# The first layer of a softplus feed-forward network by Strassen's scheme over pairs of weight tiles

## The chip, the cores and the metric

The kernel runs on one core of a Trainium2 chip. Its engines are named as the profile names them: PE is TensorE's matmul stream and PEld its weight loads, DVE is VectorE, ACT is ScalarE, POOL is GpSimd, and SP is the engine whose queue issues the transfers. Each engine works its own instructions off in the order in which they were written, and waits on semaphores for the others. The metric is the time of one execution on the device in microseconds (us).

## What is computed

Eight batches of 576 tokens go through a decaying causal attention without softmax (8 heads of 64), and the result through a feed-forward network with softplus between its layers:

```
scores = q @ k.T / sqrt(64);  ret = scores * gamma[h] ** (i - j) for i >= j, else 0
x = (ret @ v) as 4608 tokens x 512
h = x @ w_in            # 512 -> 2048, the first layer
g = max(h, 0) + log1p(exp(-abs(h)))
out = g @ w_out         # 2048 -> 512, the second layer
```

The weights arrive as 64-bit floats, two 32-bit words each.

## The kernel before

**Numbers in two parts.** Every operand of the two layers is held as a high part (the value as float32r) and a low part (what that leaves), and each product is the sum of three: low by high, high by low, high by high (`TERMS`).

**Units and slots.** The tokens form 9 units of 512 (`T`). A unit has 16 slots, one for each tile of 128 of the 2048 hidden values. In slot i, `hidden_mm` (L367) multiplies 12 times 512 columns: four pieces of the 512 inputs, three terms. ACT then takes Abs, Exp and Ln (L375 to L377), DVE adds the positive part (L383, L387), ACT writes the high part of g (L391) and DVE its low part (L395). `output_mm` (L407) of the slot before multiplies 12 times 512 columns, three for each of the four groups of 128 tokens (banks y0 to y3). So PE has 24 products of 512 columns in a slot, and each slot's elementwise work has the time of the slot after it.

**Attention.** A step m is half the heads of a chunk of 128 tokens. The first nine steps run in an opening of some 23 us. The others lie between the slots: up to slot 18 one step in every odd slot, then one chunk (two steps, `chunk_products`) ahead of every fourth slot. DVE scales what comes out (`values_out`, L346), ACT writes its high part and POOL its low part into the unit's input tile (L351, L352). POOL also scales the next step's v (`scale_values`, L151) once its transfer (`load_step`, tiles keys and qv) has landed.

**Weights.** In the 16 slots of unit 0 the two halves of each tile's weights are loaded, joined to float32 (L440, L447, L453) and split into high and low (L461, L466). They then stay in the core's memory, so that from unit 1 on nothing is loaded but attention's inputs.

**Order.** The order of the instructions is written out by hand, and each engine follows it. Tiles come from pools with a fixed number of buffers; a new tile waits until the last reader of its buffer's former tile is done.

## Time and profile before

| what | value |
|---|---|
| median of 3 timed runs | 892.06 us (892.0 to 892.66) |
| span of the profiled execution | 890.1 us |
| PE busy | 879.6 us (99%), 7634 matmuls |
| DVE, ACT, POOL busy | 460.1 (52%), 440.6 (49%), 144.1 us (16%) |
| products of the first layer (L367) | 1740, of 12 a slot |
| products of the second layer (L407) | 1728 |
| read and written in the chip's main memory (HBM) | 59.26 MB and 9.44 MB |

The profiled execution has no time of its own beside its span, which lacks 1.96 us to the median. Matmuls overlap, so the mean duration of one (391 ns) is longer than the distance between two; distances are read from rows of the timeline.

### The profile page before, as it was taken

To read this page: it belongs to the slowest core of one execution; us is meant where nothing else is said; L and a number is where in the kernel's file an instruction comes from. 1 tells how busy PE (TensorE), PEld (TensorE's weight loads), DVE (VectorE), ACT (ScalarE), POOL (GpSimd) and SP (SyncE) were. 2 spreads that over 40 slices of the span, in tenths; PEclk is the share of its full clock that TensorE was granted. 3 is DMA by queue.
4 is the path that set the end of the run, shared out by engine and by line. 5 is a ranking of instruction groups with operands and counts; after the bars stand their busy time and mean duration, and the time that the engine had idled before them with its cause. 6 is when DMAs were issued, how large, how long until landed. Compare 5 with 4: busy or idle time off the path is not lost.

```text
span 890.1 us, 18133 instructions
## 1 busy us (share of the span) xinstructions
PE 879.6 (99%) x7634; PEld 723.8 (81%) x7634; DVE 460.1 (52%) x875; ACT 440.6 (49%) x771; POOL 144.1 (16%) x265
## 2 busy tenths in 40 slices
PE   8999999999999999999999999999999999999998
PEld 6777778888888888888888888888888888888886
DVE  5898864445444454455444454444444544434333
ACT  6777854444544454444444454444444544444444
POOL 4221222111111111111111111111111111000000
PEclk9999999999999999999999999999999999999999
DMA  9666623111310121112111131012111211001001
GB/s 364 193 216 221 218 69 113 54 55 54 102 47 23 41 101 54 55 55 101 55 54 54 55 102 54 26 41 90 54 54 54 101 55 54 2 1 48 0 1 48
DMA packets 29313, 69.86 MB, mean 78 GB/s; under 512 B 3248, under 2 KB 3248, under 8 KB 29232
## 3 DMA queue, kind: packets, MB, share of 16 engines
q1 hardware_dynamic: 29232, 68.71, 22.9%
q8 instruction: 60, 0.98, 0.5%
q14 instruction: 21, 0.17, 0.1%
HBM read 59.26 MB, written 9.44 MB: 77 GB/s over the span
## 4 chain that ended last, share of the span: by engine, by line
PE 93%; DVE 3%; ACT 1%; DMA 1%; issue 0%; SPq 0%; DVEq 0%
PE h L367 43%; PE y L407 42%; PE sums L174 2%; PE bank L158 2%; PE bank L230 2%; PE bank L242 1%; DVE w L466 1%; DMA raw<-whole 1%; DVE g L395 1%; PE pair L290 1%; DMA wst<-w 1%; PE bank L327 0%; PE bank L305 0%; ACT ab L377 0%; ACT ab L376 0%
## 5 line engine op out<-in xcount | busy, mean ns | idle before, releaser
L367 PE MATMUL h<-xt,w 128*128 128x512 f32 (+1 forms) x1740 | 420.5, 391 | 1.9 <-DVE w L466 1.3
L407 PE MATMUL y<-w,g 128*128 128x512 f32 x1728 | 415.9, 390 | 1.2 <-DVE g L395 1.2
L407 PEld LDWEIGHTS y<-w,g 128*128 128x128 f32 x1728 | 323.7, 188 | 71.0 <-DVE g L395 4.0
L367 PEld LDWEIGHTS h<-xt,w 128*128 128x128 f32 x1740 | 322.1, 188 | 70.0 <-DVE w L466 1.7
L375 ACT ACTIVATE ab<-h 128x512 f32<-128x512 f32 (+1 forms) x145 | 86.3, 595 | 252.0 <-PE h L367 252.0
L383 DVE TENSOR_SCALAR r<-h 128x512 f32<-128x512 f32 x125 | 86.4, 692 | 211.1 <-ACT ab L375 211.1
L391 ACT CAST g<-ab 128x512 fp32r<-128x512 f32 (+1 forms) x145 | 89.5, 617 | 106.1 <-DVE ab L387 104.9
L395 DVE TENSOR_TENSOR g<-ab,g 128x512 fp32r<-128x512 f32 (+1 forms) x145 | 103.1, 711 | 69.4 <-ACT g L391 68.0
L352 POOL TENSOR_TENSOR xt<-x,xt 128x256 fp32r<-128x256 f32 x71 | 54.2, 780 | 519.7 <-ACT xt L351 519.7
L387 DVE SCALAR_TENSOR_TENSOR ab<-r,ab 128x512 f32<-128x512 f32 x125 | 89.4, 715 | 79.6 <-ACT ab L377 79.6
L376 ACT ACTIVATE ab<-ab 128x512 f32<-128x512 f32 (+1 forms) x145 | 91.2, 629 | 4.6
L377 ACT ACTIVATE ab<-ab 128x512 f32<-128x512 f32 (+1 forms) x145 | 91.2, 629 | 4.7
L351 ACT CAST xt<-x 128x256 fp32r<-128x256 f32 x72 | 27.1, 405 | 56.8 <-DVE x L346 55.4
L151 POOL TENSOR_TENSOR qv<-qv,consts_sb 128x256 f32<-128x256 f32 x61 | 41.3, 676 | 52.0 <-DMA qv<-others 51.6
L225 POOL TENSOR_TENSOR s<-s,consts_sb 128x128 f32<-128x128 f32 x55 | 24.2, 440 | 62.3 <-DVE s L223 50.1
L158 PE MATMUL bank<-qv,keys 64*64 64x64 f32 x976 | 34.0, 222 | 0.0
L346 DVE TENSOR_TENSOR x<-bank,consts_sb 128x256 f32<-128x256 f32 x64 | 24.6, 419 | 17.8 <-PE sums L174 12.3
L174 PEld LDWEIGHTS sums<-qv,keys 64*64 64x64 f32 x768 | 26.5, 134 | 8.5 <-issue 8.5
L230 PE MATMUL bank<-a,qv 64*64 64x64 f32 x976 | 32.9, 218 | 0.0
L158 PEld LDWEIGHTS bank<-qv,keys 64*64 64x64 f32 x976 | 29.4, 134 | 3.5 <-issue 3.5
L174 PE MATMUL sums<-qv,keys 64*64 64x64 f32 x768 | 32.0, 221 | 0.0
L230 PEld LDWEIGHTS bank<-a,qv 64*64 64x64 f32 x976 | 29.9, 135 | 0.4 <-issue 0.4
(84 smaller groups left out, 444.2 us busy)
## 6 DMA issues: line engine op xcount, KB each, us to landing
qv<-others SPq DMA_DIRECT2D x61, 320.0 KB, 4.1
wst<-w SPq DMA_DIRECT2D x32, 512.0 KB, 4.2
keys<-others SPq DMA_DIRECT2D x61, 256.0 KB, 3.5
out<-osb SPq DMA_DIRECT2D x36, 256.0 KB, 2.4
raw<-whole SPq DMA_DIRECT2D x7, 512.0 KB, 8.3
raw<-others SPq DMA_DIRECT2D x3, 576.0 KB, 10.7
part<-first SPq DMA_DIRECT2D x1, 512.0 KB, 3.7
part<-first SPq DMA_DIRECT2D x1, 262.0 KB, 2.7
```

What stands on the lines that cost most here:

```text
L158: nc.tensor.matmul(L["S"][rows[t], h, part[s]], L["k"][rows[h], s, part[t]], L["q"][rows[h], s, part[t]], start=True, stop=True, skip_grou ...
L174: nc.tensor.matmul(L["T"][rows[h], t, part[s]], L["kp"][rows[t], s, rows[h]], L["v"][rows[t], s, rows[h]], start=True, stop=True, skip_gro ...
L230: nc.tensor.matmul(L["O"][rows[h], t, part[s]], L["v"][rows[t], s, rows[h]], L["a"][rows[t], h, s], start=clear, stop=L["states"][t] is No ...
L367: nc.tensor.matmul(h, ws[p][:, a, kt * P:(kt + 1) * P], xt[:, b, kt, cols], start=(n == 0), stop=(n == 3 * NKT - 1))
L375: nc.scalar.activation(ab, h, AF.Abs)
L376: nc.scalar.activation(ab, ab, AF.Exp, scale=-1.0)
L377: nc.scalar.activation(ab, ab, AF.Ln, bias=1.0)
L383: nc.vector.tensor_scalar_max(r, h, 0.0)
L387: nc.vector.scalar_tensor_tensor(ab, h, 0.0, ab, op0=ALU.max, op1=ALU.add)
L391: nc.scalar.copy(g[:, HI], ab)
L395: nc.vector.tensor_sub(g[:, LO], ab, g[:, HI].bitcast(F32))
L407: nc.tensor.matmul(y, g[:, a, at:at + P], ws[p][:, b, PIECE:], start=(p == 0 and n == 0), stop=(p == NF - 1 and n == 2))
```

## The change

From unit 1 on, the first layer is no longer computed slot by slot, but for pairs of hidden tiles (64 pairs J, 8 for each unit) by Strassen's scheme in Winograd's form. The weights of a pair form 2 by 2 blocks (256 inputs by 128 hidden values), the unit's inputs 2 by 2 blocks (256 inputs by 256 tokens). Instead of 8 block products there are 7, each of 6 matmuls of 256 columns (two pieces of inputs, three terms): 42 matmuls of 256 columns where two slots had 24 of 512. Three of the sums are gathered by accumulating several products in one PSUM bank; between them ACT copies the partial sum out (`keep`) and DVE adds two of them into halves of two tiles hs, from which Abs, Exp and Ln now read. The output products of the former pair stand between the seven, in four portions (`fill_in`).

- **Inputs.** From unit 1 on, seven of the eight combinations of a chunk's halves are formed by POOL (`combined_out`), and ACT and POOL split all seven at once (`x_head`, `x_rest`).
- **Weights.** In unit 0 each joined first-layer tile is also written to a scratch in HBM (`plain`). In the last slot of unit 0 and during the first seven pairs of unit 1, two such tiles are read back into one buffer f (`combine_load`), combined by four POOL operations (`combine`), split by ACT and DVE in three groups ga, gb, gc (`combine_split`) and written to another scratch (`combined`). The pair that follows uses the blocks from where they were split. From unit 2 on, the blocks of a pair are read from the scratch two pairs ahead (`block_load`): 7 blocks of 256 KB, 1.8 MB a pair, into two buffers for each group.
- **The rest.** The separate positive part (L383) goes. The second layer's products, attention's products and their number stay as they were. The last slot is no longer cut in two.

What stands in the engines' queues, at three places. Rows name tiles without their numbers where they can be told without.

ACT in unit 1, before, two slots (ab and g are the elementwise tiles, h a PSUM bank):

```order
L375 ACTIVATE ab<-h 128x512 [waits PE_49]
L376 ACTIVATE ab<-ab 128x512 [waits Activation_49]
L377 ACTIVATE ab<-ab 128x512 [waits Activation_49]
L391 CAST g<-ab 128x512 [waits DVE_49]
L375 ACTIVATE ab<-h 128x512 [waits PE_49]
L376 ACTIVATE ab<-ab 128x512 [waits Activation_49]
L377 ACTIVATE ab<-ab 128x512 [waits Activation_49]
L391 CAST g<-ab 128x512 [waits DVE_49]
```

and with the change, one pair of unit 1 (kept are the copied sums, hx and hy the two PSUM banks, f the pair of weight tiles being combined, ga, gb, gc its groups):

```order
L717 COPY kept<-hx 128x256 [waits PE_49]
L717 COPY kept<-hy 128x256 [waits PE_49]
L546 CAST ga__1927<-f 128x768 [waits DMAHW6_49,DMAHW1_49,Pool_49]
L717 COPY kept<-hx 128x256 [waits DVE_49,PE_49]
L722 ACTIVATE ab<-hs 128x512 [waits DVE_49]
L723 ACTIVATE ab<-ab 128x512 [waits Activation_49]
L724 ACTIVATE ab<-ab 128x512 [waits Activation_49]
L546 CAST gb__1960<-f 128x512 [waits DMAHW7_49,Pool_49]
L431 CAST g<-ab 128x512 [waits DVE_49,PE_49]
L546 CAST gc__1980<-f 128x512 [waits DMAHW3_49,DMAHW0_49,Pool_49]
L787 COPY hs<-hx 128x4x64 [waits PE_49]
L722 ACTIVATE ab<-hs 128x512 [waits Activation_49]
```

The three casts from f stand between the copies and the logarithms of the pair, and behind POOL and the transfers.

DVE at the same place, before, two slots:

```order
L383 TENSOR_SCALAR r<-h 128x512 [waits Activation_49]
L387 SCALAR_TENSOR_TENSOR ab<-r,ab 128x512 [waits DVE_49,Activation_49]
L395 TENSOR_TENSOR g<-ab,g 128x512 [waits Activation_49]
L383 TENSOR_SCALAR r<-h 128x512 [waits Activation_49]
L387 SCALAR_TENSOR_TENSOR ab<-r,ab 128x512 [waits DVE_49,Activation_49]
L395 TENSOR_TENSOR g<-ab,g 128x512 [waits PE_49,Activation_49]
```

and with the change, the same pair:

```order
L752 TENSOR_TENSOR hs<-hy,kept 128x4x64 [waits Activation_49]
L435 TENSOR_TENSOR g<-ab,g 128x512 [waits DVE_49]
L376 TENSOR_TENSOR xb<-bank,consts_sb 128x256
L209 TENSOR_TENSOR a<-bank,mask 128x256
L547 TENSOR_TENSOR ga__1927<-f,ga__1927 128x768 [waits DMAHW6_49,DMAHW1_49,Activation_49]
L763 TENSOR_TENSOR hs<-hy,kept 128x4x64 [waits PE_49,Activation_49]
L547 TENSOR_TENSOR gb__1960<-f,gb__1960 128x512 [waits Activation_49]
L769 TENSOR_TENSOR hs<-hx,kept 128x4x64 [waits PE_49]
L427 SCALAR_TENSOR_TENSOR ab<-hs,ab 128x512 [waits DVE_49]
L547 TENSOR_TENSOR gc__1980<-f,gc__1980 128x512 [waits DMAHW3_49,DMAHW0_49,Activation_49]
L435 TENSOR_TENSOR g<-ab,g 128x512 [waits DVE_49]
```

The low parts of the three groups stand between the additions that empty the PSUM banks (the rows that write hs) and the softplus.

SP and POOL around the same pair; before, SP's loads of two steps and POOL's work for a chunk:

```order
L137 DMA keys<-others 128x512 [waits DMAHW5_49,DMAHW1_49,PE_49]
L140 DMA qv<-others 128x640 [waits DMAHW6_49,Pool_49]
L137 DMA keys<-others 128x512 [waits DMAHW3_49,PE_49]
L140 DMA qv<-others 128x640 [waits DMAHW0_49,Pool_49]
L137 DMA keys<-others 128x512 [waits DMAHW5_49,PE_49]
L140 DMA qv<-others 128x640 [waits DMAHW2_49,Pool_49]
```

```order
L352 TENSOR_TENSOR xt_1691<-x,xt_1691 128x2x128 [waits Activation_49] x2
L207 COPY sx<-s 64x128 [waits PE_49,Pool_49]
L225 TENSOR_TENSOR s<-s,consts_sb 128x128 [waits DVE_49,Pool_49]
L207 COPY sx<-s 64x128 [waits PE_49,Pool_49]
L225 TENSOR_TENSOR s<-s,consts_sb 128x128 [waits DVE_49,Pool_49]
L151 TENSOR_TENSOR qv<-qv,consts_sb 128x256 [waits DMAHW0_49]
L151 TENSOR_TENSOR qv<-qv,consts_sb 128x256 [waits DMAHW2_49,PE_49]
```

with the change, SP (wf is the scratch of plain tiles, the first three rows write the combined groups) and POOL:

```order
L548 DMA ga_125<-ga__1927 128x1536 [waits DMAHW2_49,DVE_49]
L548 DMA gb_126<-gb__1960 128x1024 [waits DMAHW3_49,DVE_49]
L548 DMA gc_127<-gc__1980 128x1024 [waits DMAHW4_49,DVE_49]
L529 DMA f<-wf_109 128x512 [waits DMAHW5_49,Pool_49]
L530 DMA f<-wf_110 128x256 [waits DMAHW6_49]
L531 DMA f<-wf_110 128x256 [waits DMAHW7_49]
L155 DMA keys<-others 128x512 [waits DMAHW0_49,PE_49]
L158 DMA qv<-others 128x640 [waits DMAHW1_49]
L155 DMA keys<-others 128x512 [waits DMAHW2_49,PE_49]
L158 DMA qv<-others 128x640 [waits DMAHW3_49]
```

```order
L243 TENSOR_TENSOR s<-s,consts_sb 128x128 [waits DVE_49] x2
L169 TENSOR_TENSOR qv<-qv,consts_sb 128x256 [waits DMAHW1_49,PE_49]
L169 TENSOR_TENSOR qv<-qv,consts_sb 128x256 [waits DMAHW3_49,PE_49]
L538 TENSOR_TENSOR f<-f 128x256 [waits DMAHW7_49,DMAHW6_49,Activation_49]
L538 TENSOR_TENSOR f<-f 128x256 [waits DMAHW5_49,Pool_49]
L538 TENSOR_TENSOR f<-f 128x256 [waits Pool_49]
L538 TENSOR_TENSOR f<-f 128x256
```

The reads into f now stand on SP behind the write of group gc and ahead of the loads of the next attention steps, and POOL's combining stands behind the scaling of v, which waits for those loads.

The diff, cut to its core:

```diff
+B11, B22, B21, T1, T3, T2, NT4 = range(7)
+GROUPS = {"ga": 3, "gb": 2, "gc": 2}
+A11, A12, S1 = (("ga", n) for n in range(3))
+S2, S4 = (("gb", n) for n in range(2))
+S3, A22 = (("gc", n) for n in range(2))
+FA21, FA11, FA12, FS1, FS2, FS4, FS3, FA22 = range(8)
+FGROUPS = {"ga": slice(1, 4), "gb": slice(4, 6), "gc": slice(6, 8)}
...
+    rawp, xpools, wpool, gpool = pool("rawp", 2), [pool("xeven", 1)], pool("wpool", 1), pool("gpool", 2)
...
+    plain = [dram.tile([P, PIECE], I32, name=f"wf{p}") for p in range(NF)]
+    combined = [{g: dram.tile([P, 2, n, 2 * P], F32R, name=f"{g}{j}") for g, n in GROUPS.items()} for j in range(NJ)]
...
+            shape = [P, 2, 7, 2, HT] if u else [P, 2, NKT, T]
+            xts[u] = xpools[u % 2].tile(shape, F32R, tag="xt", name=f"xt{u}")
...
+    def halves_out(m):
+        L = live.pop(m)
+        pr = 2 * (m % 2)
+        if m % 2 == 0:
+            xbs[0] = att.tile([P, 8, 2, HC], F32, tag="xb", name="xb", bufs=1)
+        nc.vector.tensor_mul(xbs[0][:, pr:pr + 2], L["O"].rearrange("p t (s c) -> p t s c", s=2),
+                             constant[0][2][:, pr:pr + 2].rearrange("p s (t c) -> p t s c", t=2))
+    def combined_out(m, engine):
+        xb = xbs[0]
+        if m % 2 == 0:
+            engine.tensor_sub(xb[:, 4], xb[:, 0], xb[:, 1])
+        else:
+            engine.tensor_sub(xb[:, 5:7], xb[:, 2].unsqueeze(1).broadcast_to([P, 2, 2, HC]), xb[:, 0:5:4])
+            engine.tensor_sub(xb[:, 7], xb[:, 3], xb[:, 6])
...
+    def x_head(ch):
+        nc.scalar.copy(x_parts(ch)[0], xbs[0][:, 1:8])
+    def x_rest(ch, engine):
+        hi, lo = x_parts(ch)
+        engine.tensor_sub(lo, xbs[0][:, 1:8], hi.bitcast(F32))
...
-        nc.vector.scalar_tensor_tensor(hi, hi, 3, lo, op0=ALU.logical_shift_left, op1=ALU.bitwise_or)
+        if n % 2 == 0:
+            full = wst.tile([P, PIECE], I32, tag="full", name="full", bufs=2)
+            nc.vector.scalar_tensor_tensor(full, hi, 3, lo, op0=ALU.logical_shift_left, op1=ALU.bitwise_or)
+            nc.sync.dma_start(plain[n // 2], full)
     def weight_dst(n):
-        cols = slice((n % 2) * PIECE, (n % 2 + 1) * PIECE)
-        return ws[n // 2][:, HI, cols], ws[n // 2][:, LO, cols]
+        p = n // 2
+        if n % 2:
+            return wouts[p][:, HI], wouts[p][:, LO]
+        if p not in wins:
+            wins[p] = gpool.tile([P, 2, PIECE], F32R, tag=("gb", "gc")[p % 2], name=f"win{p}")
+        return wins[p][:, HI], wins[p][:, LO]
+    def combine_load(j):
+        f = later["f"].tile([P, 8, 2 * P], I32, tag="f", name="f")
+        nc.sync.dma_start(f[:, FA11:FA12 + 1].rearrange("p b c -> p (b c)"), plain[2 * j])
+        nc.sync.dma_start(f[:, FA21], plain[2 * j + 1][:, 0:2 * P])
+        nc.sync.dma_start(f[:, FA22], plain[2 * j + 1][:, 2 * P:])
+        fulls["f", j] = f.bitcast(F32)
+    def combine(j):
+        f = fulls["f", j]
+        for out, a, op, b in ((FS1, FA21, nc.gpsimd.tensor_add, FA22), (FS2, FS1, nc.gpsimd.tensor_sub, FA11),
+                              (FS4, FA12, nc.gpsimd.tensor_sub, FS2), (FS3, FA11, nc.gpsimd.tensor_sub, FA21)):
+            op(f[:, out], f[:, a], f[:, b])
+    def place_block(j, g):
+        blocks[j, g] = gpool.tile([P, 2, GROUPS[g], 2 * P], F32R, tag=g, name=f"{g}_")
+        return blocks[j, g]
+    def combine_split(j, g):
+        f, t = fulls["f", j][:, FGROUPS[g]], place_block(NJ + j, g)
+        nc.scalar.copy(t[:, HI], f)
+        nc.vector.tensor_sub(t[:, LO], f, t[:, HI].bitcast(F32))
+        nc.sync.dma_start(combined[j][g].bitcast(F32), t.bitcast(F32))
+    def block_load(J, g):
+        if NJ * 2 <= J < NPAIRS:
+            nc.sync.dma_start(place_block(J, g).bitcast(F32), combined[J % NJ][g].bitcast(F32))
...
+    for i in range(NF):
...
+        if i == NF - 1:
+            combine(0)
...
+        def step_out():
+            halves_out(m - 1)
+            combined_out(m - 1, nc.vector if i == NF - 1 else nc.gpsimd)
             scores_out(m)
             states_out(m)
-            for k in (m + 1,) if i < by_chunks - 2 else (m + 1, m + 2):
-                load_step(k)
...
+            if m + 1 >= NOPEN:
+                load_step(m + 1)
+            scale_values(m + 1)
+        def parts_out():
+            if (m - 1) % 2:
+                x_head((m - 1) // 2)
+                x_rest((m - 1) // 2, nc.vector if i == NF - 1 else nc.gpsimd)
+        if i == NF - 1:
+            step_out()
+            parts_out()
...
-            for name, bufs in (("osb", 4), ("odd", 2), ("r", 1), ("mark", 2)):
+            for name, bufs in (("osb", 3), ("odd", 2), ("f", 1), ("mark", 2)):
                 later[name] = ctx.enter_context(tc.tile_pool(name=name + "2", bufs=bufs, side="right"))
+            combine_load(0)
+        if i == NF - 1:
+            for g in GROUPS:
+                combine_split(0, g)
+            combine_load(1)
...
+    groups = {NJ: ([m + 1], [m])}
+    m += 2
+    for J in (J for J in range(NJ + 1, NPAIRS) if J % NJ in ((1, 2, 4, 5) if J < 2 * NJ else (0, 2, 4, 5))):
+        groups[J] = [k for k in (m, m + 1) if k < NSTEP], [k for k in (m - 2, m - 1) if k >= groups[NJ][0][0]]
+        m += 2
...
+    def product(out, J, a, x, start):
+        g, n = a
+        w = blocks[J, g]
+        k = 0
+        for ta, tb in TERMS:
+            for kt in range(2):
+                nc.tensor.matmul(out, w[:, ta, n, kt * P:(kt + 1) * P], x_tile(J // NJ)[:, tb, x, kt],
+                                 start=start and k == 0, stop=k == 5, skip_group_check=True)
+                k += 1
...
+    def keep(part):
+        kept = moe.tile([P, HT], F32, tag="kept", name="kept")
+        nc.scalar.copy(kept, part)
+        return kept
...
+    late, last = [], None
+    for J in range(NJ, NPAIRS):
+        u, j = divmod(J, NJ)
+        if J == NJ:
+            fills = [[(NF - 1, (tt,))] for tt in range(CPU)]
+        else:
+            fills = [[(2 * J - 2, (0, 1))], [(2 * J - 2, (2, 3))], [(2 * J - 1, (0, 1))], [(2 * J - 1, (2, 3))]]
...
+        prep = u == 1 and j + 1 < NJ
+        tile_a, tile_b = (moe.tile([P, T], F32, tag="hs", name="hs") for _ in range(2))
+        if prep:
+            combine(j + 1)
+        X = ps_h.tile([P, T], F32, tag="h0", name="hx")
+        Y = ps_h.tile([P, T], F32, tag="h1", name="hy")
+        x0, y0, y1 = X[:, 0:HT], Y[:, 0:HT], Y[:, HT:]
+        product(x0, J, A11, B11, True)
+        p1 = keep(x0)
+        product(y1, J, A12, B21, True)
+        product(y0, J, S1, T1, False)
+        block_load(J + 2, "ga")
+        p5 = keep(y0)
+        nc.vector.tensor_add(half(tile_a, 1), by_chunk(y1), by_chunk(p1))
+        for f in late:
+            f()
+        late = []
+        if prep:
+            combine_split(j + 1, "ga")
+        fill_in(0)
+        product(x0, J, S2, T2, False)
+        u2 = keep(x0)
+        product(y0, J, S4, B22, False)
+        block_load(J + 2, "gb")
+        nc.vector.tensor_add(half(tile_a, 0), by_chunk(y0), by_chunk(u2))
+        ab = hidden_logs(tile_a)
+        if prep:
+            combine_split(j + 1, "gb")
+        fill_in(1)
+        product(x0, J, S3, T3, False)
+        nc.vector.tensor_add(half(tile_b, 0), by_chunk(x0), by_chunk(p5))
+        softplus(tile_a, ab)
+        if last is not None:
+            x_head(last)
+            x_rest(last, nc.gpsimd)
+            last = None
+        ga = softplus_split(ab)
+        gs[2 * J] = ga
+        if prep:
+            combine_split(j + 1, "gc")
+        fill_in(2)
...
+        product(x0, J, A22, NT4, False)
+        block_load(J + 2, "gc")
+        if u == 1 and j + 2 < NJ:
+            combine_load(j + 2)
+        nc.scalar.copy(half(tile_b, 1), by_chunk(x0))
+        softplus_rest(ga, ab)
+        if J in groups:
+            steps, done = groups[J]
+            chunk_products(steps, done)
+            for m in steps:
+                states_out(m)
+            def outs(steps=steps, done=done):
+                for m in done:
+                    halves_out(m)
+                    combined_out(m, nc.gpsimd)
+                for m in steps:
+                    scores_out(m)
+            late.append(outs)
+            if done and done[-1] % 2:
+                last = done[-1] // 2
+            for m in steps:
+                for k in (m + 1, m + 2) if J == NJ else (m + 2,):
+                    if k < NSTEP:
+                        load_step(k)
+                        scale_values(k)
+        fill_in(3)
...
+        ab = hidden_logs(tile_b)
+        softplus(tile_b, ab)
+        gb = softplus_split(ab)
+        gs[2 * J + 1] = gb
+        late.insert(0, lambda g=gb, ab=ab: softplus_rest(g, ab))
+    for f in late:
+        f()
+    output_mm(2 * J)
+    output_mm(2 * J + 1)
```

159 lines of the change are left out of this document (69 added, 90 removed).

## The prediction, made before the change was run

> **What bounds the kernel now.** I read the page's shares first, then the windows, which give the busy time of each engine in a stretch (the column behind the length is PE's), then the timeline for the distances.
>
> ```profile
> PE 879.6 (99%) x7634; PEld 723.8 (81%) x7634; DVE 460.1 (52%) x875; ACT 440.6 (49%) x771; POOL 144.1 (16%) x265
> ...
> 47.00:72.00 25.00, 24.59 (x224) 19.40 (x223) 22.74 (x43) 19.45 (x34) 6.43 (x8) 1.00 0.63 216
> 142.00:238.00 96.00, 96.00 (x869) 79.54 (x868) 47.07 (x93) 43.31 (x73) 16.16 (x29) 1.00 0.19 61
> ```
>
> From unit 1 on PE is busy in all of the 96 us; ACT and DVE have half of each stretch free. In unit 0 (47 to 72 us) DVE is at 91% and PE just short of full. So the time is PE's stream, and its unit is the distance between two products:
>
> ```profile
> 123.31 2.88 PE L367 MATMUL h<-xt,w 128*128 128x512 f32 x12
> ...
> 126.03 2.88 PE L407 MATMUL y<-w,g 128*128 128x512 f32 x12
> ...
> 877.44 3.05 PEld L367 LDWEIGHTS h<-xt,w 128*128 128x128 f32 x24
> 877.66 3.04 PE L367 MATMUL h<-xt,w 128*128 128x256 f32 x24
> ...
> L367 PE MATMUL h<-xt,w x24: 278/283/283, 877.7 to 880.4; 128*128 128x256 f32 x24
> ```
>
> Twelve products of 512 columns take 126.03 - 123.31 = 2.72 us, 0.2267 each. The last slot happens to run the very form that the change uses, 24 times 256 columns: its last start is 3.04 - 0.283 behind its first, over 23 distances, 0.120 us each. Half of 0.2267 would be 0.113, so a product of half the width has 0.007 us of its own.
>
> **The gain.** A pair had 24 x 0.2267 = 5.44 us of first-layer products and gets 42 x 0.120 = 5.04. That is 0.40 us a pair, 25.6 us over 64 pairs; with the last slot's 24 x 0.120 back in, 25.8. The output products stay 5.44, so a pair goes from 10.88 to 10.48 us. The gain is 3% of the layer's arithmetic and no more, so that any wait of 0.4 us a pair eats it.
>
> One rule weighed against these rows: the Trainium skill, "TensorE: Matmul & The Clock Gate", section "Back-to-back issue gap", gives N/2.4 + 2.5 ns. By it 256 columns would take an estimated 109 ns and 512 some 216, and the gain would be 0.59 us a pair, 38 us; the rows show 120 and 227, and the rows are used.
>
> **Units 2 to 8: does the elementwise work keep up?** Durations (busy, mean ns) by form:
>
> ```profile
> L395 DVE TENSOR_TENSOR g<-ab,g 128x512 fp32r<-128x512 f32 x143 | 102.3, 715 | 67.3 <-ACT g L391 65.9 <-PE bank L174 0.7
> L387 DVE SCALAR_TENSOR_TENSOR ab<-r,ab 128x512 f32<-128x512 f32 x125 | 89.4, 715 | 79.6 <-ACT ab L377 79.6
> L391 ACT CAST g<-ab 128x512 fp32r<-128x512 f32 x143 | 88.7, 620 | 104.9 <-DVE ab L387 104.9
> L391 ACT CAST g<-ab 128x256 fp32r<-128x256 f32 x2 | 0.8, 399 | 1.2 <-PE y L407 1.2
> L346 DVE TENSOR_TENSOR x<-bank,consts_sb 128x256 f32<-128x256 f32 x64 | 24.6, 419 | 17.8 <-PE sums L174 12.3 <-PE bank L242 5.5
> L151 POOL TENSOR_TENSOR qv<-qv,consts_sb 128x256 f32<-128x256 f32 x61 | 41.3, 676 | 52.0 <-DMA qv<-others 51.6
> L352 POOL TENSOR_TENSOR xt<-x,xt 128x256 fp32r<-128x256 f32 x71 | 54.2, 780 | 519.7 <-ACT xt L351 519.7
> ...
> 210.15 0.60 ACT L375 ACTIVATE ab<-h 128x512 f32<-128x512 f32 x1 [2.13 <-PE h L367]
> 210.78 0.63 ACT L376 ACTIVATE ab<-ab 128x512 f32<-128x512 f32 x1
> 211.45 0.63 ACT L377 ACTIVATE ab<-ab 128x512 f32<-128x512 f32 x1
> 212.84 0.62 ACT L391 CAST g<-ab 128x512 fp32r<-128x512 f32 x1 [0.76 <-DVE ab L387]
> ```
>
> From Abs to the end of the cast the chain takes 212.84 + 0.62 - 210.15 = 3.31 us, 1.96 of them up to the softplus. In the new order the tightest loop runs from the last product (A22): 0.16 us drain, copy of 256 columns 0.40, the chain 3.31, the next pair's first copy 0.40, some 0.15 for hand-overs: 4.4 us. PE meanwhile has fill 3 (1.36), three products (2.16) and fill 0 (1.36), 4.88 us. It holds, by 0.4. ACT then has about 6.6 us of 10.48 and DVE 4.2. Attention's POOL work is longer than before (three subtractions and a low part of 896 columns, some 3.8 us, where L352 took 1.56), and ACT's split of the seven combinations waits for it; if the loads land 1 us later than now, ACT is 0.8 us late in the three of eight pairs that follow a chunk and are followed by none. I take 2 us in all, bounds 0 and 14 (0.8 x 3 x 6 units). The block reads, 1.8 MB in 10.48 us, are 175 GB/s, below the 216 GB/s of the unit 0 row, where the distance of output products was 0.2267 too.
>
> **Unit 1 is another matter.** There the blocks are made, and f has one buffer. So this loop must run once for each of the seven pairs, and it holds no PE work: end of the low part of gc, write of gc and reads of f; POOL's first combination; cast of ga; low part of ga; addition into hs; Abs, Exp, Ln; cast of gb (behind Ln on ACT); low part of gb; the addition that frees the bank hx (behind it on DVE); softplus; cast of g; cast of gc; low part of gc. Two things in it hold PE: ACT's cast of ga, behind which the copy out of hx is queued that the product S3 waits for, and the addition, which A22 waits for. From the rows: POOL 0.72 (between 676 and 780 ns); casts of 768 columns 0.84 and of 512 0.62 (0.22 for each 256 more); low parts 0.97 and 0.70; additions 0.42; 1.96 for the logarithms; 0.71 softplus; 0.62 cast; 0.04 at each change of engine. Sum behind the reads: 0.72 + 0.88 + 1.01 + 0.42 + 1.99 + 0.66 + 0.74 + 0.42 + 0.71 + 0.66 + 0.62 + 0.73 = 9.6 us.
>
> ```profile
> wst<-w SPq DMA_DIRECT2D x32, 512.0 KB, 4.2
> ...
> 190.70 0.33 SPq L137 DMA_DIRECT2D keys<-others  x1
> 191.12 0.38 SPq L140 DMA_DIRECT2D qv<-others  x1
> 191.60 0.38 SPq L137 DMA_DIRECT2D keys<-others  x1
> 192.07 0.38 SPq L140 DMA_DIRECT2D qv<-others  x1
> ...
> 197.47 0.87 POOL L151 TENSOR_TENSOR qv<-qv,consts_sb 128x256 f32<-128x256 f32 x1 [1.88 <-DMA qv<-others]
> ...
> 189.50 0.16 DVE L280 COPY mark<-sums 128x1 f32<-128x1 f32 x1 [0.71 <-PE sums L174]
> 213.51 0.16 DVE L280 COPY mark<-sums 128x1 f32<-128x1 f32 x1 [0.70 <-PE sums L174]
> ```
>
> The reads: 512 KB take 4.2 us; here they are three issues, 0.46 apart, behind the write of another 512 KB. I take 4.6, bounds 3.9 and 5.6. The loop is 14.2 us (13.5 to 15.2), more than PE's 10.48. Behind a chunk it is worse: POOL combines only after it has scaled two v's, whose four loads SP issues behind the write and the three reads. The chunk's products end when the low part of gc does (both 2.8 us after the addition, by 0.72 and 2.0 of products and by 0.71 + 0.66 + 0.62 + 0.73), so its loads come right behind the reads. Now, from the first of four issues (190.70) to the end of the second scaling (197.47 + 0.87) it is 7.64 us; four issues ahead add 1.85. So POOL is free 9.5 us after the low part of gc (bounds 7.8, the loads not delayed, and 10.9, their 1 MB in the way as well), and the loop is 19.1 us (17.4 to 20.5). Chunks lie in pairs 0, 1, 2, 4 and 5, so five of the seven loops are of this kind.
>
> Sum: 2 x 14.2 + 5 x 19.1 + 1.5 (two output copies and writes ahead of the second read) = 125.4 us; unit 1's first seven pairs last 0.75 us longer than the loops (1.35 ahead of the first, less 0.6 at the end), 126.2. Without waits they are 7.76 for the first (its output products are half) and 6 x 10.48, 70.6, and attention: a chunk costs 213.51 - 189.50 - 4 x 5.44 = 2.25 us, three and two small ones 10.0. Together 80.6. PE waits 45.6 us; with the low bounds 34, with the high ones 56.
>
> **Smaller terms.** Into unit 1, by the clock of before:
>
> ```profile
> 117.80 0.68 DVE L466 TENSOR_TENSOR w<-wst,w 128x512 fp32r<-128x512 f32 x1
> 118.57 0.69 DVE L395 TENSOR_TENSOR g<-ab,g 128x512 fp32r<-128x512 f32 x1
> ...
> 120.59 2.88 PE L407 MATMUL y<-w,g 128*128 128x512 f32 x12
> ...
> 103.06 0.92 POOL L352 TENSOR_TENSOR xt<-x,xt 128x256 fp32r<-128x256 f32 x1
> 103.30 1.23 DVE L466 TENSOR_TENSOR w<-wst,w 128x512 fp32r<-128x512 f32 x1
> ```
>
> PE would want its first block product at 123.31. DVE is through with slot 14 at 119.26; then scale, two combinations, mask and two state sums (2.1, by L346's 0.42 for 256 columns), ACT's split of 896 columns and DVE's low part (to 122.6); ACT's logarithms begin at 121.5, softplus, cast and ga's two parts end at 126.7. PE waits 3.4 (2.5 to 5). In unit 0 POOL has some 2 us more for each chunk, and DVE stretches under POOL (the low part of a weight 1.23 us at 103.30, 0.68 at 117.80): 2 us over four chunks (0.5 to 5). At the end the last pair's softplus is late for the last twelve products: 4.7 us of chain against 4.1 of PE work, 0.6 (0.3 to 1). The writes of plain tiles cost nothing: SP waits there anyway for DVE, who frees the next load; without that cover 0.46 us a slot, 7 us.
>
> 890.1 - 25.8 + 45.6 + 3.4 + 2.0 + 0.6 + 2.0 = 917.9 us of span, and with the 1.96 that the median lies above the span, **920 us**. All low bounds: 904; all high ones: 947.
>
> **Rivals.** (1) *Faster: the loop of unit 1 doesn't hold PE.* Then 874. It decides at a mean loop of 14.0 us, (80.6 + 17.8 - 0.75) / 7, where PE's waits are 17.8 us and the sum is zero; mine is 17.9. For it: the reads land in 2.5 us and the loads don't delay POOL. Against: in-order queues, and 9.6 us in the loop before any transfer. 0.17. (2) *Units 2 to 8 wait too*, ACT behind POOL behind the loads, at every one of the 24 chunks left: 24 x 0.8 = 19, 939. For: ACT's split ends as the copy of A22 wants to begin. Against: the loop's 4.4 under 4.88 us. 0.11. (3) *The clock falls in unit 1's gaps.* Two waits of 2 to 3 us a pair.
>
> ```profile
> 5.09:8.51 3.42, 1.72 (x43) 1.12 (x39) 1.38 (x2) 2.31 (x9) 0.00 (x0) 1.00 1.01 373
> 8.51:11.92 3.41, 3.41 (x50) 2.58 (x48) 1.94 (x5) 2.24 (x10) 1.53 (x3) 0.50 1.03 422
> ```
>
> After a stretch with PE busy 1.72 of 3.42 us the granted clock was 0.50 for 3.4 us. That costs PE 1.7 us of work, which the loop hides except for the chunk's products ahead of the loads: 5 x 1.7, 928. 0.07. The Trainium skill, "TensorE: Matmul & The Clock Gate", section "What's actually happening", puts the fall after a whole idle window of some 3.4 us; by it nothing would fall here, while this trace shows it after half of one. (4) *Weight loads come to stand between the products.* By the rows, 2688 products would each take 0.192 + 0.120, 1436 us. Against: in the 24 products each load of 192 ns lies under its neighbours, at 120 a pair of both. 0.01. The Trainium skill, "TensorE: Matmul & The Clock Gate", section "The mechanism", lets loads overlap only products on other rows of the array and so speaks for this rival; this trace doesn't agree.
>
> **Chances.** The forecast has 0.59; with (2) to (4) slower has 0.78. Faster by more than 0.2% (1.8 us, about what can be told from no change) has 0.17, within it 0.05, which is a mean loop near 14.0 us, as it would be if the chunks' loads didn't delay POOL at all. The forecast's own range is 904 to 942, with not all high bounds at once; 892 to 942 leaves out rival (1) and the upper part of (2), 0.2 together.
>
> **What would show it.** Right: PE idle only between some 127 and 255 us, by 40 us or so, released by DVE's additions and ACT's copies; ACT's cast of ga waiting for POOL by 2 to 6 us a pair; PE full from unit 2 on, at 10.5 us a pair. Wrong: a loop under 14 us; distances of 256-column products other than 0.120; PE idle in unit 3 or later.

## The result, and the profile after

The changed kernel takes 947.38 us (median of 4 runs, 944.56 to 949.56) where the kernel before took 892.36 beside it: a ratio of 1.061, interval 1.059 to 1.064. It is slower, by 55 us; the forecast was 920, with a range of 892 to 942. The profiled execution, the slowest of the four, took 949.56 us, with a span of 947.9.

The page after: shares, PE's busy time in 40 slices of 23.7 us, and the clock granted to PE in the same slices.

```profile
PE 890.8 (94%) x8774; PEld 777.7 (82%) x8774; DVE 514.1 (54%) x968; ACT 544.2 (57%) x1015; POOL 251.5 (27%) x358
...
PE   8999977777889999999999999999999999999997
...
PEclk9999997789779999999999999999999999999999
```

PE was at 99% and is at 94%; the dip lies in slices 6 to 12, which is the end of unit 0 and unit 1, and the clock dips there as well. The windows, by stage (length, then busy time of PE, its loads, DVE, ACT and POOL, the granted clock, the DMA share and GB/s): slots 0 to 15, the first seven pairs of unit 1, the eighth, units 2 to 7, unit 8.

```profile
24.01:131.71 107.70, 97.40 (x852) 76.71 (x852) 95.46 (x168) 78.96 (x131) 32.06 (x42) 1.00 0.69 220
131.71:274.79 143.08, 108.23 (x970) 90.67 (x971) 66.53 (x119) 58.76 (x109) 54.80 (x72) 0.79 0.52 184
274.79:285.60 10.81, 10.81 (x67) 9.65 (x67) 4.99 (x9) 7.04 (x14) 0.00 (x0) 0.99 0.63 223
285.60:852.10 566.50, 563.70 (x6002) 505.09 (x6000) 298.34 (x582) 329.98 (x613) 154.16 (x222) 1.00 0.65 214
852.10:947.90 95.80, 90.65 (x553) 80.41 (x551) 35.64 (x62) 54.41 (x103) 0.00 (x0) 1.00 0.43 143
```

The first block product starts at 131.71 us, where the first product of unit 1 started at 123.31 before: 8.4 us are lost by then. Seven pairs take 143.08 us; without waits they would take 80.6 by the prediction's count. In the 566 us of units 2 to 7 PE is idle for less than 3. A plain pair there (no attention in it) lasts 10.56 us from its first product to the next pair's. The balance of the spans, 947.9 - 890.1 = 57.8:

| part | forecast | measured |
|---|---|---|
| fewer products, 64 pairs | -25.8 | -20.7 (64 x (10.88 - 10.56), and 0.2) |
| unit 0 and the step into unit 1 | +5.4 | +8.4 |
| unit 1, seven pairs | +45.6 | +61.9 (143.08 - 80.6 - 7 x 0.08) |
| the rest of units 1 to 8 and the end | +2.6 | +8.2 (what is left) |
| sum | +27.8 | +57.8 |

The 0.08 us are what a pair's products take longer than forecast (10.56 for 10.48); they are counted in the first row.

What PE waits for in 24 to 290 us, the view of waits (releaser, us in all, times, longest):

```profile
PE hx L704 <- ACT kept L717: 20.3, 7, 4.5
PE hx L704 <- DVE hs L769: 11.4, 7, 2.8
PE h L413 <- DVE win L516: 5.0, 4, 1.3
PE hx L704 <- DVE ga__1700 L547: 3.7, 1, 3.7
```

The first two are the two places that the prediction named: the product S3 behind the copy out of hx, which stands in ACT's queue behind the cast of ga, and A22 behind the addition, which stands in DVE's queue behind the low part of gb. Each waits seven times, once for each pair that makes blocks. The fourth is the step into unit 1.

One round of the loop, in pair 10, from the low part of gc to the next low part of gc (the timeline: start, us, engine, line, output and input, and in brackets the idle time before it and its releaser):

```profile
170.01 0.69 DVE L547 TENSOR_TENSOR gc__1980<-f,gc__1980 128x512 fp32r<-128x512 f32 x1 [1.26 <-ACT gc__1980 L546]
...
171.14 1.43 SPq L529 DMA_DIRECT2D f<-wf  x1
...
173.62 0.38 SPq L155 DMA_DIRECT2D keys<-others  x1
...
174.99 0.43 SPq L158 DMA_DIRECT2D qv<-others  x1
...
178.69 0.61 POOL L169 TENSOR_TENSOR qv<-qv,consts_sb 128x256 f32<-128x256 f32 x1 [3.22 <-PE hx L704]
...
181.25 0.61 POOL L169 TENSOR_TENSOR qv<-qv,consts_sb 128x256 f32<-128x256 f32 x1 [1.95 <-DMA qv<-others]
181.82 3.75 POOL L538 TENSOR_TENSOR f<-f 128x256 f32<-128x256 f32 x4
182.58 0.83 ACT L546 CAST ga__2130<-f 128x768 fp32r<-128x768 f32 x1 [5.62 <-POOL f L538]
183.32 0.37 ACT L717 COPY kept<-hx 128x256 f32<-128x256 f32 x1
...
183.74 1.65 PE L704 MATMUL hx<-xt,gc__1980 128*128 128x256 f32 x6 [2.98 <-ACT kept L717]
184.90 0.41 DVE L763 TENSOR_TENSOR hs<-hy,kept 128x256 f32<-128x256 f32 x1
...
188.72 2.09 POOL L399 TENSOR_TENSOR xt<-xb,xt 128x896 fp32r<-128x896 f32 x1 [1.92 <-ACT xt L395]
188.78 2.58 DVE L427 SCALAR_TENSOR_TENSOR ab<-hs,ab 128x512 f32<-128x512 f32 x1
...
192.68 0.69 DVE L547 TENSOR_TENSOR gc__2182<-f,gc__2182 128x512 fp32r<-128x512 f32 x1 [1.31 <-issue]
```

The round takes 192.68 - 170.01 = 22.67 us, where the forecast had 19.1. Two stretches of it are to be told apart. From the end of gc's low part (170.70) to POOL's first combination (181.82) it is 11.1 us: write of gc, reads of f, four loads, and the two scalings that wait for them. From there to the end of the next low part (193.37) it is 11.55 us, where the forecast had 9.6; 1.87 of the 1.95 on top is the softplus on DVE, forecast at 0.71, which takes 2.58 us beside POOL's low part of seven combinations and 0.68 elsewhere.

By the same rows the seven rounds take 15.6, 21.5, 22.7, 23.4, 14.7, 21.5 and 22.2 us, 141.6 in all, where the forecast had 125.4. Of the 16.2 between them, 7.8 lie in the four rounds with a softplus of 2.58 us, 1.95 in each; 6.6 are the transfers behind a chunk (11.9, 11.1, 11.9, 10.0 and 10.7 us, for five times 9.5 and 1.5); 1.9 are the two rounds without a chunk.

### The profile page after: what moved, and what is told of

It is laid out like the page before. It is cut to its first block, busy times and chain, and to the rows that moved or that the text cites. A ratio compares the mean times of both kernels' runs of the same rounds, so it can differ in the third digit from the quotient of the medians.

```text
span 947.9 us, 21655 instructions
## 1 busy us (share of the span) xinstructions
PE 890.8 (94%) x8774; PEld 777.7 (82%) x8774; DVE 514.1 (54%) x968; ACT 544.2 (57%) x1015; POOL 251.5 (27%) x358
## 4 chain that ended last, share of the span: by engine, by line
PE 66%; ACT 2%; DVE 2%; DMA 1%; POOL 1%; issue 1%; SPq 0%; DVEq 0%; ACTq 0%; POOLq 0%
PE y L444 32%; PE hx L704 17%; PE hy L704 13%; PE sums L192 1%; DVE g L435 1%; PE bank L176 1%; PE bank L248 1%; PE bank L260 1%; DMA qv<-others 1%; ACT g L431 0%; ACT xt L395 0%; POOL qv L169 0%; ACT ab L722 0%; ACT ab L723 0%; ACT ab L724 0%
## 5 line engine op out<-in xcount | busy, mean ns | idle before, releaser
L444 PE MATMUL y<-wout,g 128*128 128x512 f32 x1728 | 455.2, 401 | 1.9 <-DVE g L435 1.9
L444 PEld LDWEIGHTS y<-wout,g 128*128 128x128 f32 x1728 | 312.7, 192 | 60.2 <-DVE g L435 4.8
L431 ACT CAST g<-ab 128x512 fp32r<-128x512 f32 x144 | 89.3, 620 | 135.6 <-DVE ab L427 130.6
L435 DVE TENSOR_TENSOR g<-ab,g 128x512 fp32r<-128x512 f32 x144 | 136.7, 949 | 40.1 <-ACT g L431 39.4
L427 DVE SCALAR_TENSOR_TENSOR ab<-hs,ab 128x512 f32<-128x512 f32 x128 | 96.6, 754 | 47.2 <-ACT ab L724 46.2
L722 ACT ACTIVATE ab<-hs 128x512 f32<-128x512 f32 x128 | 80.9, 632 | 68.8 <-DVE hs L763 67.1
L724 ACT ACTIVATE ab<-ab 128x512 f32<-128x512 f32 x128 | 81.0, 633 | 4.1
L723 ACT ACTIVATE ab<-ab 128x512 f32<-128x512 f32 x128 | 80.9, 632 | 4.1
L752 DVE TENSOR_TENSOR hs<-hy,kept 128x256 f32<-128x256 f32 x64 | 27.2, 425 | 97.9 <-ACT kept L717 97.9
L399 POOL TENSOR_TENSOR xt<-xb,xt 128x896 fp32r<-128x896 f32 x31 | 66.8, 2156 | 43.8 <-ACT xt L395 43.8
L413 PE MATMUL h<-xt,win 128*128 128x512 f32 x192 | 47.4, 395 | 5.7 <-DVE win L516 5.0
L763 DVE TENSOR_TENSOR hs<-hy,kept 128x256 f32<-128x256 f32 x64 | 26.9, 421 | 33.3 <-PE hy L704 31.5
```

Source lines behind the costliest of these rows:

```text
L399: engine.tensor_sub(lo, xbs[0][:, 1:8], hi.bitcast(F32))
L413: nc.tensor.matmul(h, wins[p][:, a, kt * P:(kt + 1) * P], xt[:, b, kt, cols], start=(n == 0), stop=(n == 3 * NKT - 1))
L427: nc.vector.scalar_tensor_tensor(ab, h, 0.0, ab, op0=ALU.max, op1=ALU.add)
L431: nc.scalar.copy(g[:, HI], ab)
L435: nc.vector.tensor_sub(g[:, LO], ab, g[:, HI].bitcast(F32))
L444: nc.tensor.matmul(ys[u][tt], g[:, a, tt * P:(tt + 1) * P], wouts[p][:, b], start=(p == 0 and n == 0), stop=(p == NF - 1 and n == 2))
```

## The experiments

The theory (A) is the prediction's: a loop through the single buffer f, which holds next to no PE work, sets the length of a pair in unit 1. The rivals are that the scheme is slow by itself (B), that transfers or elementwise work are the bound whatever the buffers (C), and that the half clock lengthens the pairs (D). Ratios are to runs of the kernel before beside them, whose medians were 892.7 to 893.3 us.

### Without the making of the blocks

```diff
-        if NJ * 2 <= J < NPAIRS:
-            nc.sync.dma_start(place_block(J, g).bitcast(F32), combined[J % NJ][g].bitcast(F32))
+        if NJ < J < NPAIRS:
+            nc.sync.dma_start(place_block(J, g).bitcast(F32), combined[0][g].bitcast(F32))
...
-        prep = u == 1 and j + 1 < NJ
+        prep = False
```

> Blocks 1 to 7 are not made: unit 1 and every later unit read the eight pairs' blocks from the scratch of block 0, so the output is left wrong for pairs 1 to 7, with the same products, the same reads and the same attention. Theory A (the single buffer f and its chain hold PE in unit 1, and nothing else of the change costs much): the first seven pairs of unit 1 fall from 143 us to some 81, the granted clock stays at 1.00 there, and the time is 947 - 62 = 885 us. Theory B (the scheme itself is slow: units 2 to 8 or the products of 256 columns cost what was lost): the time stays above 920.

This kernel leaves out the combining, splitting and writing of blocks 1 to 7. Measured: 896.51 us, ratio 1.004 (1.002 to 1.005); making the blocks costs 51 us. That is most of the loss, as A has it, but 885 was expected. The seven pairs:

```profile
132.56:223.48 90.92, 85.49 (x970) 76.58 (x971) 47.52 (x99) 47.10 (x88) 29.27 (x43) 0.95 0.75 254
```

They take 90.9 us, not 81. Most of the difference is in pair 9, 19.3 us long for 12.8. There PE waits 4.3 us for the copy of hx, which is behind a cast, behind a softplus, behind DVE's copy of the last output tile of unit 0; that copy waits 5.34 us for one of the three output buffers to be written out:

```profile
148.90 0.69 DVE L454 COPY osb<-y 128x512 f32<-128x512 f32 x1 [5.34 <-DMA out<-osb]
149.51 0.68 DVE L427 SCALAR_TENSOR_TENSOR ab<-hs,ab 128x512 f32<-128x512 f32 x1
```

In the changed kernel the same copy waits too, 2.16 us, under the loop. So B holds in part: even with its blocks for nothing, this layout is not faster than the kernel before, since the products give 20.7 us and the way into unit 1, its outputs and the pairs behind chunks take as much.

### POOL's order

```diff
         if prep:
             combine(j + 1)
+        for k in scales:
+            scale_values(k)
+        scales = []
...
                         load_step(k)
-                        scale_values(k)
+                        scales.append(k)
```

> POOL combines the next pair's tiles before it scales the two v's of a chunk, where it scaled first. Theory A with POOL's order as the larger part (POOL stands behind 1.2 MB of loads that queue behind the f reads, five times): the five loops behind a chunk fall from 21.5 to 23.4 us by some 5 to 6 each, and the time by 25 to 30, to 917 to 922 us. Rival C (the f reads themselves are what lands late, since the transfers of 3.5 MB a pair are the bound): under 8 us, 940 or more.

Measured: 924.03 us, ratio 1.033 (1.032 to 1.035), 23 us less than the changed kernel. POOL in pair 10 now:

```profile
171.74 3.51 POOL L538 TENSOR_TENSOR f<-f 128x256 f32<-128x256 f32 x4 [1.91 <-ACT kept L717]
175.22 1.90 POOL L169 TENSOR_TENSOR qv<-qv,consts_sb 128x256 f32<-128x256 f32 x2
```

The rounds behind a chunk fall to between 16.1 and 20.1 us and the seven pairs to 122.2. The gain is nearly the one expected; C, by which the reads of f themselves are late, is ruled out for this part. POOL's order alone cost 23 us: the combining, which PE needed, stood in an in-order queue behind a scaling that waited for its load.

### POOL's long instruction beside DVE

```diff
-        engine.tensor_sub(lo, xbs[0][:, 1:8], hi.bitcast(F32))
+        for a, b in ((0, 2), (2, 4), (4, 6), (6, 7)):
+            engine.tensor_sub(lo[:, a:b], xbs[0][:, 1 + a:1 + b], hi[:, a:b].bitcast(F32))
```

> POOL takes the low part of the seven combinations in four instructions (2, 2, 2 and 1 of them) where it took one of 2.1 us; nothing else moves. Theory E (DVE stands still until the POOL instruction that is under way has ended, so one of 2.1 us makes a DVE operation of 0.7 last 2.1 to 2.6): DVE's stretched operations fall to 1.3 us or less, the four waits in unit 1 by about 1.3 us each, the second of two chunks in a row in units 2 to 8 from 13.5 to 13.0 us a pair, and the three waits of 1.4 us in unit 0 by half: 947 falls by 8 to 13 us, 934 to 939. Rival F (the stretch is a matter of both engines' bandwidth, whatever the length of one instruction): 945 or more.

Measured: 937.78 us, ratio 1.051 (1.050 to 1.053), 9.6 us less. The same softplus and POOL's low part, in pair 10:

```profile
188.50 1.21 DVE L428 SCALAR_TENSOR_TENSOR ab<-hs,ab 128x512 f32<-128x512 f32 x1
```

```profile
188.44 2.97 POOL L400 TENSOR_TENSOR xt<-xb,xt 128x256 fp32r<-128x256 f32 x4 [1.93 <-ACT xt L395]
```

DVE waits for the end of one POOL instruction, not for the whole stretch, and POOL's four together take longer (2.97 for 2.09), since DVE now gets in between. In units 2 to 7 the pair of the second of two chunks in a row falls from 13.40 to 12.69 us on the mean. Theory E holds there, F does not. In unit 0 the pieces did less than expected: PE's three waits fell from 1.34, 1.27 and 1.14 us to 0.83, 1.14 and 1.06, not to half. The other way to take the overlap away, in unit 1 alone:

```diff
-            x_rest(last, nc.gpsimd)
+            if u == 1:
+                rest_of = last
+            else:
+                x_rest(last, nc.gpsimd)
...
         softplus_rest(ga, ab)
+        if rest_of is not None:
+            x_rest(rest_of, nc.vector)
```

> In unit 1 the low part of the seven combinations is taken by DVE behind the low part of the first tile, not by POOL beside DVE's softplus, which takes 2.58 us under it and 0.68 without. Theory A with this stretch in the loop: four pairs (10, 11, 13, 14) lose 1.9 us each and pay at most 1.2 us of DVE time for it off the loop, 939 to 942 us. If the stretch is not on the path: 947.

Measured: 941.07 us, ratio 1.053 (1.050 to 1.057), as expected. The softplus in pair 10 takes 0.68 us, and DVE does the whole low part in 1.08:

```profile
189.22 0.68 DVE L427 SCALAR_TENSOR_TENSOR ab<-hs,ab 128x512 f32<-128x512 f32 x1
...
192.43 1.08 DVE L399 TENSOR_TENSOR xt<-xb,xt 128x896 fp32r<-128x896 f32 x1
```

### The half clock

```diff
+    def keep_busy(X, J, count):
+        if J < 2 * NJ - 1:
+            w, x = blocks[J, "gc"], x_tile(J // NJ)
+            for k in range(count):
+                nc.tensor.matmul(X[:, HT:], w[:, HI, 0, 0:P], x[:, HI, B22, 0], start=False, stop=True,
+                                 skip_group_check=True)
...
+        keep_busy(X, J, 22)
         product(x0, J, S3, T3, False)
...
+        keep_busy(X, J, 22)
         product(x0, J, A22, NT4, False)
```

> 22 products of 256 columns into the unused half of the bank hx, ahead of product S3 and again ahead of A22, in the first seven pairs of unit 1: PE works in the waits and its clock should stay nearer to 1.00. Theory A (the loop, which holds no PE work, sets the pair): the half clock is a companion of the waits and the time stays within 4 us of 947. Rival D (the half clock, 56 us of unit 1, itself lengthens the pairs): with the clock up the time falls by 10 to 25 us.

Measured: 958.96 us, ratio 1.075 (1.070 to 1.080), 12 us more than the changed kernel. By itself this decides little. The added products write the bank hx, so they wait for its copy and its addition as S3 and A22 do: they stand behind PE's waits and not in them, 5.3 us a pair (pair 12, 18.1 us, is full from end to end). In the profiled execution, which took 968.18 us, 9 more than the median, the seven pairs take 142.5 us, as without them, while units 2 to 7 take 583.8 where they took 566.5, with the loads of a chunk landing later; why they do was not settled. So the same with 10:

> The changed kernel with 10 products of 256 columns (1.2 us) into the unused half of the bank hx ahead of S3 and of A22 in the first seven pairs of unit 1, 22 before: they fit into waits of some 3 us. Theory A (the loop, which holds no PE work but the chunk's products, sets the pair): the time stays within 5 us of 947, whatever the clock does. Rival D (the half clock lengthens the pairs): if the half clock falls from 56 us by half or more, the time falls by 8 us or more.

Measured: 946.54 us, ratio 1.060 (1.057 to 1.062). The seven pairs:

```profile
130.83:271.81 140.98, 112.36 (x1111) 98.28 (x1111) 66.52 (x119) 59.06 (x109) 54.79 (x72) 0.92 0.53 186
```

and the first ten added products of pair 10, behind their wait:

```profile
182.02 1.94 PE L731 MATMUL hx<-xt,gc__2010 128*128 128x256 f32 x10 [2.61 <-ACT kept L717]
```

The granted clock in unit 1 went from 0.79 to 0.92, which is 60 us of half clock down to 23 (twice the missing share, by the length), and the time stayed where it was, within 1 us. Since the added products come behind the waits, their own 1.2 us could have hidden a gain; two readings speak against it. From POOL's first combination to the end of gc's low part the seven rounds take 9.5, 9.6, 11.5, 11.6, 9.6, 11.6 and 11.5 us in the changed kernel, and with the added products each is the same within 0.05. And SP's loads of the chunks' inputs wait for PE by 1.0 us in all in unit 1 of the changed kernel, so PE's pace hardly reaches the transfers. D is ruled out as the cause of the loss: PE works slowly in stretches in which the loop would have it wait anyway.

### Two buffers

```diff
+        f = later["f"].tile([P, 4, 2 * P], I32, tag="f", name="f")
+        s = fulls["s", j] = later["fs"].tile([P, 3, 2 * P], F32, tag="fs", name="fs")
...
+            for name, bufs in (("f", 2), ("fs", 1)):
...
         if prep:
             combine_split(j + 1, "gb")
+            combine_split(j + 1, "gc")
+            if j + 2 < NJ:
+                combine(j + 2)
+            if j + 3 < NJ:
+                combine_load(j + 3)
```

> The four plain tiles have two buffers, the three sums one (11 KB instead of 8, one output buffer less in unit 1); a pair's tiles are read two pairs ahead and combined one pair ahead, and ACT splits ga, gb and gc where POOL is through long before. The computation is the same. Theory A (the chain over the single buffer holds PE): the seven pairs fall from 143 us to 85 to 92 (81 without any wait), the half clock goes, and the time to 890 to 897 us. Rival C (transfers of 3.5 MB a pair, or DVE and POOL with some 12 us of work in a chunk's pair, are the bound whatever the buffers): the pairs stay above 14 us on the mean, 905 or more.

Measured: 919.02 us, ratio 1.030 (1.029 to 1.032); the seven pairs take 114.0 us. 28 us are gone, but 85 to 92 us for the seven pairs were expected, and the 905 or more that C was to give came out. The 28 us are not the second buffer's alone: the edit also takes POOL's combining out from behind the scaling (what pair 10 splits is combined from 161.80 us on, the scalings follow at 170.92), and that by itself, with the one buffer, had given 23. The waits of the next kernel (below) show that the rest isn't C. Two buffers and POOL's low part in pieces together:

> Both edits together, two buffers and the low part in four instructions. If they add up: 880 to 888 us, and faster than the kernel before (893). If the two buffers leave no wait for DVE in unit 1, the pieces give only their part in units 0 and 2 to 8, some 5 us below the two buffers alone.

Measured: 912.23 us, ratio 1.022 (1.020 to 1.023), 6.8 less than the two buffers alone. They add up in units 0 and 2 to 8 only; unit 1 keeps its 114 us. What PE waits for in it:

```profile
PE hx L714 <- DVE hs L785: 13.8, 6, 2.9
PE hx L714 <- ACT kept L727: 3.7, 1, 3.7
PE hx L714 <- DVE ga__1718 L553: 3.2, 1, 3.2
```

Now it is the addition in six pairs and the copy in one, and DVE's rows ahead of it in pair 10 say why (of the kernel with two buffers):

```profile
173.70 0.41 DVE L773 TENSOR_TENSOR hs<-hy,kept 128x256 f32<-128x256 f32 x1
176.65 0.69 DVE L552 TENSOR_TENSOR gb__2173<-fs,gb__2173 128x512 fp32r<-128x512 f32 x1 [2.53 <-ACT gb__2173 L550]
177.26 0.69 DVE L552 TENSOR_TENSOR gc__2177<-f,gc__2177 128x512 fp32r<-128x512 f32 x1
177.86 0.42 DVE L784 TENSOR_TENSOR hs<-hx,kept 128x256 f32<-128x256 f32 x1
```

DVE stands still for 2.5 us, since its next instruction is the low part of gb, whose cast is queued on ACT behind three logarithms; the addition that PE needs, whose product S3 ended at 174.89, comes third. The round through f was only one of two locks: the place of the low parts in DVE's queue was the other, worth 13.8 us of PE's waits, 2.3 in each of six pairs.

### Queues reordered

```diff
         ab = hidden_logs(tile_a)
         if prep:
-            combine_split(j + 1, "gb")
-            combine_split(j + 1, "gc")
+            combine_rests(j + 1, "ga")
+            combine_store(j + 1, "ga")
+            combine_heads(j + 1, "gb")
+            combine_heads(j + 1, "gc")
...
         softplus(tile_a, ab)
+        if prep:
+            for g in ("gb", "gc"):
+                combine_rests(j + 1, g)
+                combine_store(j + 1, g)
...
         if i == NF - 1:
-            step_out()
+            halves_out(m - 1)
+            combined_out(m - 1, nc.vector)
             parts_out()
+            combine_heads(0, "ga", slice(0, 1))
+            combine_rests(0, "ga", slice(0, 1))
```

> The kernel with two buffers and pieces, and its queues reordered: DVE takes the low parts of ga behind the addition that frees the bank hy, those of gb and gc behind the addition that frees hx and behind the softplus (they stood ahead of them and waited for ACT's casts); in the first pair of unit 1 each output tile goes out behind its own last product; into unit 1 the first two blocks are split ahead of the last slot's logarithms. Theory A' (what is left of unit 1's waits is DVE held in order behind ACT's casts, 2.8 us a pair): the seven pairs fall from 114 us to 84 to 92, the first block product comes at 126 to 127 us where it came at 128.9, and the time is 880 to 890 us. Rival C (transfers, or DVE and POOL together, are the bound): the pairs stay above 100 us, 898 or more.

Measured: 887.81 us, ratio 0.995 (0.993 to 0.997). This version is faster than the kernel before, by 0.3 to 0.7%, and 60 us faster than the change as it was made. It is 24 us below the two edits together; DVE's order is the main part, but the outputs of unit 0 and the first two blocks were moved forward as well.

```profile
126.51:217.72 91.21, 85.83 (x970) 75.23 (x971) 65.61 (x133) 60.93 (x120) 60.32 (x84) 0.98 0.78 282
```

The first block product comes at 126.51 us, the seven pairs take 91.2, PE is busy for all but 5.4 of them and the clock is at 0.98. PE now waits for the addition 0.3 us and for the copy 1.0 us in all of them. The same transfers now run at 282 GB/s in place of 184, and DVE, ACT and POOL each do some 60 to 66 us of work in the 91. So C is ruled out for the change as made: neither the transfers nor the elementwise work was the bound there. The rest of the way to 80.6 wasn't taken apart further.

### Two tries at the products of the second layer

A fill of six of them takes, in the changed kernel, from its start to the start of what follows 373.44 - 372.06 = 1.38 us, 0.231 each, where they took 0.227 before the change:

```profile
372.06 1.55 PE L444 MATMUL y<-wout,g 128*128 128x512 f32 x6
373.44 0.88 PE L704 MATMUL hx<-xt,gb__3964 128*128 128x256 f32 x6
```

```diff
-            wouts.append(pool.tile([P, 2, PIECE], F32R, name=f"wout{len(wouts)}"))
+            n = 2 if len(wouts) % 2 == 0 and len(wouts) + 1 < upto else 1
+            t = pool.tile([P, 2, n, PIECE], F32R, name=f"wout{len(wouts)}")
+            wouts.extend(t[:, :, k] for k in range(n))
```

> As the kernel before it, and the high and low tiles of the second layer's weights lie 4096 bytes apart, as they did before the change, and not 2048. In the traces a product of the second layer takes 0.227 us before the change and 0.231 after it (0.228 to 0.236 in a fixed pattern of six), in every unit. If the place of the two tiles is the cause: 0.227 again, 24 x 0.0046 = 0.11 us a pair, 7 us less than the kernel beside it. If not: the same time within 2 us.

```diff
     nc.vector.memset(fill, 1.0)
+    nc.vector.memset(moe.tile([P, HT], F32, tag="kept", name="kept"), 0.0)
```

> The reordered kernel with the two buffers of g 2048 bytes further on, where they lie as before the change with regard to 4096 bytes (35264 and 39360; before the change 31168 and 35264; after it 33216 and 37312); nothing else differs. If the place of the second layer's stationary tiles makes its products take 0.231 us for 0.227: 0.227 again, 0.11 us a pair, some 7 us in all, 881. If not: 888 within 2.

Measured: 888.62 us (ratio 0.995, 0.994 to 0.996) and 889.04 (0.995, 0.994 to 0.997), and 0.231 us a product in both. Neither place is the cause.

The traces show where the 0.0046 us lie, 0.11 us a pair and 7 us in all. The kernel before has one run of output products behind products of 256 columns, in its last slot (the first two rows): its first six take 881.92 - 880.53 = 1.39 us, 0.231 each, and the next six 0.227. The changed kernel has output products behind products of 512 columns in unit 0 (the last two rows): there twelve take 115.13 - 112.41 = 2.72 us, 0.227 each, with the layout of after, so the slower pace is not in every unit.

```profile
880.53 1.55 PE L407 MATMUL y<-w,g 128*128 128x512 f32 x6
881.92 1.52 PE L407 MATMUL y<-w,g 128*128 128x512 f32 x6
```

```profile
112.41 2.88 PE L444 MATMUL y<-wout,g 128*128 128x512 f32 x12
115.13 2.88 PE L413 MATMUL h<-xt,win 128*128 128x512 f32 x12
```

So it is not the layout: the first six output products behind products of 256 columns are slower, and the changed kernel has four such fills of six in every pair. Why they are slower stays open.

## Why the prediction was right or wrong

**Right: the direction, the place and the mechanism.** Most of the loss is in 127 to 275 us; PE waits there at the two points named, seven times each, and a plain pair of units 2 to 8 takes 10.56 us where 10.5 was said. Taking the making away gave back 51 us, and taking the loop apart (two buffers with POOL's order, then the order of the other queues) gave 28 and 24.

**Wrong: the size of the loop behind a chunk,** "the loop is 19.1 us (17.4 to 20.5)". It was 21.5 to 23.4, all five above the upper bound. Two of its terms failed:

- "0.71 softplus". It took 2.58 us in four pairs. The prediction had the row that shows it (a low part of 1.23 us under POOL, 0.68 alone) and used it for unit 0 only; it did not ask what POOL does while the loop's own DVE operations run. POOL's low part of 896 columns was in the text as a delay of ACT. The pieces and the move to DVE both gave time back, 9.6 and 6.3 us in all. (The low part of ga was stretched too, 1.53 us for a forecast of 0.97, beside POOL's combining; shorter steps around it made up for that.) The Trainium skill, "SBUF — State Buffer", section "Who interferes with whom", has the rule: a DVE instruction with two inputs in SBUF, the core's own memory, contends with a GpSimd instruction that reads SBUF, for a pair of ports that only one of them can hold; with at most one SBUF input it doesn't contend. This trace agrees with both halves: the softplus has two SBUF inputs, and the addition at 184.90, with one input in PSUM, takes 0.41 us in the middle of POOL's 3.75.
- "POOL is free 9.5 us after the low part of gc". It was 10.0 to 11.9, 11.1 on the mean, and in three of the five rounds above even the upper bound of 10.9, which had the loads' own 1 MB in the way. The value taken rests on a row of a quieter stage, where the same four loads met nothing else in the queue.

**Wrong: the bounds.** "With the high ones 56" and "all high ones: 947". The measured time lies at 947, but that is luck: PE's waits in unit 1 were 61.9 us, 6 above their high bound, and the gain was 5 us short with no bound given, while the other terms stayed 8 us below their high bounds and the median lay half a us below the profiled span, not 1.96 above it. The terms of unit 1 were too low together, in a stage with more traffic and more POOL work than the rows they were read from; that this is their common cause is likely, not shown. Terms with a common cause don't average out, so the range should have reached there. (The loops as given make the bounds 35.7 and 54.6, not 34 and 56, unless the 1.5 us for the outputs runs from 0 to 3, which the text doesn't say.)

**Wrong by 5 us: the gain.** "The output products stay 5.44". They take 5.55 (24 x 0.231), so a pair gains 0.32 us and not 0.40. A row of before had it: the last slot's first six output products, behind products of 256 columns, take 0.231 each. The products of 256 columns kept their 0.120, a little less on the mean.

**Wrong by 2.7 us: unit 0,** "2 us over four chunks". It was 4.7, the 8.4 less the wait of 3.7 for ga; 0.6 of it had passed at the first slot (24.01 us, 23.39 before). PE waits in slots 5, 9 and 13 for a weight's low part, 1.34, 1.27 and 1.14 us. Beside POOL's low part one DVE operation lasts 2.35 to 2.41 us there; with the pieces several in a row are stretched a little instead, and only 0.7 us of the three waits came back. The step into unit 1 was 3.7 where 3.4 was said.

**The rivals.** (1), that the loop doesn't hold PE, is out by the rounds. (2) appears in part: POOL's long instruction, not the loads, costs the second of two chunks in a row 0.7 us on the mean, and what follows the seven pairs loses 8 us in all. (3) happened and cost next to nothing: the clock was at one half for 60 us of unit 1, which the prediction gave one chance in fourteen, but the price it had put on it (five chunks of 1.7 us) didn't show, as the run with 10 added products says. (4) is out: each load lies under the product ahead of it, 0.120 us for both.
